# Recurrent attention with streamed weights: four stream buffers instead of six, thirteen streamed slices instead of fifteen, and three steps of the segment loop moved

## The chip, the cores and the metric

The kernel is written in Bass and Tile for Trainium2 and runs on one core. The metric is the device time of one execution in microseconds, as the median of three executions. The core has a tensor engine (PE, whose weight loads are listed apart as PEld), a vector engine (DVE), a scalar engine (ACT), GpSimd (POOL) and a sync engine (SP). SP computes nothing here: it issues the loads of the weights. ACT issues the other transfers of the loop that this document is about, between its own computations. Each engine works through its own instruction stream in order and waits on semaphores; a transfer is issued by an engine and then carried out by sixteen DMA engines.

## The reference, cut to what matters

```python
# part A: 64 segments of 32 tokens, with 8 memory rows handed from one to the next
for s in range(n_seg):                       # 2048 / 32 = 64
    h = concat([mem, x[:, 32*s:32*s+32]])    # 40 x 640
    q, k, v = h @ Wq, h @ Wk, h @ Wv         # each 640 -> 32 heads x 192
    p = softmax(mask(q @ k.T * 192**-0.5))
    o = (p @ v) @ Wo                         # 32 x 192 -> 640
    mem = o[:, :8]
    outs.append(o[:, 8:])
# part B: attention of 32 heads x 20 with a window of 8 keys, 2 apart
return g * a + (1 - g) * b                   # g = sigmoid(x . gate_w)
```

`outs` holds 40 - 8 = 32 rows a segment; the first eight rows of each segment's result are the memory of the next one. So the 64 segments form a chain: the first projection of a segment needs the last sums of the one before. The four matrices of part A (Wq, Wk, Wv and Wo, each 640 x 6144 in bf16) are needed in every segment.

## The kernel before

Three stages follow one another. **Part B** computes the windowed attention and leaves its result, already multiplied by 1 - g, in DRAM. **The prepass** (L409) computes the projections of the last eight tokens of each segment for all segments at once and leaves them in `zpk_dram`. **Part A** (L480) is the recurrence, one pass of `for s in range(nseg)` (L530) for each segment. After it `part_z` multiplies the rest of the rows by Wo.

**Weights.** Wq, Wk, Wv and Wo are cut into 80 slices of 128 x 1536 bf16, 384 KB each (`slice_keys`, L338). They don't all fit in the on-chip memory. `weights_setup` (L355) picks `N_STREAM` slices, spread evenly over an estimated time of use, that are loaded anew in every segment; the others stay resident, some loaded at the start (`wres_...`), `N_LATE` of them later (`wlate_...`). With `N_STREAM` = 15 the streamed ones are, in order of use, k(1,0), k(0,2), q(0,4), k(3,0), q(2,2), q(2,3), k(3,4), v(1,1), v(0,3), v(2,0), v(3,2), v(3,4), ob 2, ob 5 and ob 8; the numbers of q, k and v are a group of eight heads R and a chunk kc of the 640 inputs. `get_slice` (L404) loads a streamed slice through SP into one of `WBUFS` buffers (`wst`); SP issues these loads in order, and each waits until PE has done with the slice that had the buffer before. Streamed slices of Wo come from a rearranged copy in DRAM (`wscr`).

**Order.** In part A the order of PE, ACT and DVE is that of the program text (`manual_schedule`). One segment runs:

- `m_qk(0, ...)` and `m_qk(1, ...)`: q and k of head groups 0, 1 and 2, 3 with `m_dense` (L533), for each chunk kc four slices of four matmuls (a row of 32 PE columns each). Group pair 0 goes to the PSUM pairs `ps_d_5310` and `ps_d_5311`, pair 1 to `ps_d_5312` and `ps_d_5313`. After the last chunk ACT copies one pair out and DVE the other (L547).
- Between them stand parts of the previous segment. `sel_b` (L682, matmuls at L688, a copy at L692) sums chunks 2 to 4 of the next memory into `hT`, which the chunks kc = 2, 3, 4 of this segment read; chunks 0 and 1 were done by `sel("oa")` inside the previous segment. `tail` (L764, L768) forms the previous segment's output rows, `store` (L774) writes them out.
- `load_vz(s)` (L519): ACT issues the transfer of the prepass's V into `Vz`, columns 224 to 608 of the tile `ZQ`. The previous segment's `zst`, columns 32 to 416 of the same tile, is being written to `oz_dram` (L749), so this transfer has to wait for that one.
- `t_qk(0)` (L559): PE transposes q and k (L566), DVE copies Q^T (L569), ACT copies K^T (L570). Then the scores `s_a`, `s_b`, the exponentials (L602), and V with `m_v`.
- `pv_half(0)`, `pv_half(1)` (L629): attention times V, with copies by ACT and DVE at L652 and L657; `e_norm(1)` (L626, L627, on DVE) comes before `pv_half(1)`.
- `o_group(parts, i2)` (L669): the product with Wo, twelve groups of four rows of 128. Groups 0 to 5 do both column parts "oa" and "ob" (256 and 384 columns wide) at once, then 6 to 11 the part "oa", then 6 to 11 the part "ob". Groups 0 to 5 need only the first half of the heads; groups from 6 on need the copies at L652 that follow `pv_half(1)`. ACT copies the sums out at L746 ("oa") and L756 ("ob").

Of the kernel before, what the change touches and what calls it, by code (L numbers as in the profile page):

```python
# [11 lines left out]
F32 = mybir.dt.float32  # L12
I32 = mybir.dt.int32

N_STREAM = 15
N_LATE = 55
N_LATE2 = 11
WBUFS = 6

_DEV = {"mode": "full"}  # L20

# [2 lines left out]
QK = [[(m, R) for R in (2 * h, 2 * h + 1) for m in "qk"] for h in range(2)]  # L24
# [21 lines left out]
class _K:  # L46
# [308 lines left out]
    def weights_setup(self):  # L355
# [9 lines left out]
        self.stream_keys = set()  # L365
        for i in range(N_STREAM):
            left = [k for k in keys if k not in self.stream_keys]
            self.stream_keys.add(min(left, key=lambda k: abs(at[k] - (i + 0.5) * t / N_STREAM)))
        rest = [k for k in keys if k not in self.stream_keys]
# [10 lines left out]
        if so:  # L380
            scr = self.dram.tile([len(so), 128, 1536], BF, name="wscr")
            for i, k in enumerate(so):
                src, split = self.slice_info(k)
                nc.sync.dma_start(scr[i].rearrange("p (c f) -> p c f", c=split[0]), src)
                self.wscr[k] = scr[i]
        self.wstream = self.ctx.enter_context(tc.tile_pool(name="wstream", bufs=WBUFS))

# [92 lines left out]
    def part_a(self):  # L480
# [4 lines left out]
        with ctx:  # L485
# [20 lines left out]
            pairs = [psp.tile([128, 2, 512], F32, name=f"ps_d{b}") for b in range(4)]  # L506
# [11 lines left out]
            def load_vz(s):  # L518
                nc.scalar.dma_start(Vz, self.zpk_dram[s, :, 0:384])  # L519
# [10 lines left out]
            for s in range(nseg):  # L530
                pqs, sts, pSs = {}, {}, {}

                def m_dense(ks, kcs, dst):  # L533

                    for kc in kcs:
                        for x, k in enumerate(ks):
                            sl = self.get_slice((*k, kc))
                            for j in range(4):
                                mm = nc.tensor.matmul(dst[x // 2][32 * j:32 * j + 32, x % 2, 0:384], lhsT=hT[:, kc, :],  # L539
                                                      rhs=sl[:, 384 * j:384 * j + 384], start=(kc == 0),  # L540
                                                      stop=(kc == KC - 1), tile_position=(0, 32 * j),
                                                      skip_group_check=True)
                                if x:
                                    _LOADED.add(mm.ins.name)

                def copy_pair(cp, u, ps):
                    cp(KV[:, 384 * u:384 * u + 768].rearrange("p (a f) -> p a f", a=2), ps[:, :, 0:384])  # L547

                def m_qk(h, kcs):
                    dst = pairs[2 * h:2 * h + 2]  # L550
                    m_dense(QK[h], kcs, dst)
                    if kcs[-1] == KC - 1:
                        copy_pair(nc.scalar.copy, 0, dst[0])
                        copy_pair(nc.vector.tensor_copy, 2, dst[1])
# [4 lines left out]
                def t_qk(h):  # L559

                    pq, pk = (pairs[2 * h + m].bitcast(BF)[:, 0, 0:768].rearrange("p (r t f) -> p r t f", r=2, t=3)
                              for m in range(2))
                    for r in range(2):
                        for m, p in enumerate((pq, pk)):
                            for t in range(3):
                                nc.tensor.transpose(p[:, r, t, :], unit[2 * r + m][:, 128 * t:128 * t + 128],  # L566
                                                    self.ident[:])
                    blocks = lambda p: p.rearrange("p r t (j b i) -> p (r t j) b i", j=4, i=8)
                    nc.vector.tensor_copy(QTa[:, 2 - h:6 - h].rearrange("p b r c i -> p (r c) b i"), blocks(pq))  # L569
                    nc.scalar.copy(KV[:, 4 * 384:6 * 384].rearrange("p (c b i) -> p c b i", b=4, i=8), blocks(pk))  # L570
# [51 lines left out]
                def e_norm(h, rz):  # L622
                    E = Es[h]
                    EA = E[:, :, 0:80].rearrange("p a (r q) -> p a r q", q=40)
                    EB = E[:, :, 80:112].rearrange("p a (r q) -> p a r q", q=16)
                    nc.vector.tensor_tensor(out=EA, in0=EA, in1=rz, op=ALU.mult)  # L626
                    nc.vector.tensor_tensor(out=EB, in0=EB, in1=rz[:, :, :, 0:16], op=ALU.mult)  # L627
# [41 lines left out]
                def o_group(parts, i2):  # L669
                    for x, part in enumerate(parts):  # L670
                        n = 256 if part == "oa" else 384
                        for jj in range(4):
                            c = 4 * i2 + jj
                            R, j, t = c // 12, c // 3 % 4, c % 3
                            mm = nc.tensor.matmul(b_out[part][32 * jj:32 * jj + 32, 0:n],  # L675
                                                  lhsT=oTxs[2 * (R // 2) + j // 2][:, 6 * (j % 2) + 3 * (R % 2) + t, :],
                                                  rhs=o_weights(part, c), start=(c < 4), stop=(c >= 44),
                                                  tile_position=(0, 32 * jj), skip_group_check=True)
                            if x:
                                _LOADED.add(mm.ins.name)  # L680
# [12 lines left out]
                        "p (m i) -> p m i", i=8))  # L693

                m_qk(0, (0,))
                if sel_b is not None:
                    sel_b()
                if tail is not None:
                    tail()
                m_qk(0, (1, 2, 3))  # L700
                if store is not None:
                    store()
                    load_vz(s)
                m_qk(0, (4,))
                m_qk(1, (0, 1))
                t_qk(0)
                m_qk(1, (2, 3, 4))
                for chunks in (FULL, HALF):
                    s_a(0, chunks)
# [26 lines left out]
                nc.vector.tensor_copy(unit[2], pairs[3][:, 0, 0:384])  # L736
                nc.scalar.copy(unit[3], pairs[3][:, 1, 0:384])
                e_norm(1, rz)
                for i2 in range(4):
                    o_group(("oa", "ob"), i2)  # L740
                pv_half(1)
                for i2 in range(4, 6):
                    o_group(("oa", "ob"), i2)
                for i2 in range(6, 12):
                    o_group(("oa",), i2)
# [11 lines left out]
                if s + 1 < nseg:  # L757
                    def sel_b(hT_next=hT_next, sel=sel):
                        sel("ob", hT_next)

                def tail(s=s):
                    pa = pairs[2][:, 0, :]
                    for jj in range(4):
                        nc.tensor.matmul(pa[32 * jj:32 * jj + 32, 0:160], lhsT=self.sel_x[:],  # L764
                                         rhs=whi[:, 160 * jj:160 * jj + 160], start=True, stop=True,
                                         tile_position=(0, 32 * jj), skip_group_check=True)
                    g = self.gA[:, 16 * (s % 4) + s // 4:16 * (s % 4) + s // 4 + 1]
                    nc.vector.scalar_tensor_tensor(out=a4[:], in0=pa[:, 0:160], scalar=g, in1=a4[:], op0=ALU.mult,  # L768
                                                   op1=ALU.add)

                def store(s=s):
                    dst = self.out2d[32 * s:32 * s + 32, :].rearrange("t (j f) -> j t f", j=4)
                    if s + 1 < nseg:
                        nc.scalar.dma_start(dst, a4[:])  # L774
                    else:
                        for jj in range(4):
                            nc.scalar.dma_start(dst[jj, 0:24], a4[32 * jj:32 * jj + 24, :])
# [112 lines left out]
```

## Time and profile before

| | us |
|---|---|
| median of three executions | 1849.25 |
| lowest and highest | 1848.68 and 1857.12 |
| the profiled execution | 1856.27 |
| its span, first to last instruction | 1854.5 |
| part B | about 0 to 248 |
| prepass | about 248 to 435 |
| recurrence, 64 segments | about 435 to 1796 |
| `part_z` | about 1797 to 1854 |

A profile row names the engine, the line of the kernel and the operation, then the tile written and the tiles read (`ps_d_5311<-wst,hT` is a matmul of a streamed slice with the segment's input into a PSUM pair), the number of instructions and their time. What stands behind `<-` in square brackets or in the list of waits is what ended the idle time before. "issue" means that the engine waited for nothing that the profile shows. The streams named `q1`, `q10` and `q8` are the transfers that SP and ACT issue and the loading of program code.

### The profile page before, as it was taken

What the parts mean: (1) busy time and instruction counts of PE and PEld (TensorE: products, weight loads), DVE (VectorE), ACT (ScalarE), POOL (GpSimd) and SP (SyncE); (2) the same over time, 40 slices, a digit from 0 to 9 for tenths busy, and PEclk for the clock granted to TensorE, in tenths of its full rate; (3) what the DMA queues carried; (4) which work ended last, traced back from release to release, by engine and by line L of the source; (5) the groups of instructions that cost most, each with busy time, mean ns of one, the idle gap of its engine ahead of it and who ended that gap; (6) DMA issues with size and microseconds to landing.
All of it is one profiled execution on the core that took longest, in us unless ns stands there. A gap on an engine that the chain in (4) does not pass through costs nothing.

```text
span 1854.5 us, 79891 instructions
## 1 busy us (share of the span) xinstructions
PE 1642.1 (89%) x42080; PEld 751.1 (40%) x30176; DVE 781.2 (42%) x1663; ACT 766.7 (41%) x1417; POOL 41.0 (2%) x70
## 2 busy tenths in 40 slices
PE   3898898887998899998889989999888999899989
PEld 1455543332333334343333433333333333333348
DVE  2565578942333333333333443333433334333330
ACT  1675778942333333333333333333333333333340
POOL 3111000001000000000000000000000000000000
PEclk9999999998999999999999999999999999999989
DMA  9212179888999999999989998999998999899991
GB/s 279 34 44 48 33 189 284 160 169 266 312 301 303 301 312 330 313 317 307 303 301 312 319 315 293 301 311 315 312 308 284 321 311 319 296 309 313 312 298 29
DMA packets 340921, 486.15 MB, mean 262 GB/s; under 512 B 148964, under 2 KB 209892, under 8 KB 340580
## 3 DMA queue, kind: packets, MB, share of 16 engines
q1 hardware_dynamic: 198608, 419.28, 67.5%
q10 hardware_dynamic: 141972, 61.76, 14.2%
q8 instruction: 283, 4.64, 1.0%
q14 instruction: 58, 0.48, 0.1%
HBM read 446.61 MB, written 35.52 MB: 260 GB/s over the span
## 4 chain that ended last, share of the span: by engine, by line
PE 63%; DMA 15%; ACT 8%; DVE 6%; issue 6%; ACTq 2%; SPq 0%; POOL 0%; DVEq 0%
PE ps_d_5313 L539 11%; DMA oz_dram<-ZQ 10%; PE ps_d_5311 L539 9%; PE ps_d_5310 L675 6%; DVE ZS L94 5%; PE ps_d_5311 L675 5%; PE ps_d_5312 L539 5%; PE ps_bqk L240 2%; ACT bP L263 2%; PE ps_pre L441 2%; PE ps_d_5310 L539 2%; PE ps_d_5310 L566 2%; PE ps_d_5311 L821 2%; ACT KV L547 2%; PE ps_d_5312 L566 1%
## 5 line engine op out<-in xcount | busy, mean ns | idle before, releaser
L539 PEld LDWEIGHTS <-hT 128*32 128x32 bf16 x5120 | 137.6, 96 | 344.0 <-issue 246.1
L547 DVE CAST KV<-ps_d_5311 128x768 bf16<-128x768 f32 x128 | 122.6, 958 | 194.9 <-PE ps_d_5311 L539 194.9
L675 PEld LDWEIGHTS <-KV 128*32 128x32 bf16 x4608 | 131.7, 98 | 127.7 <-issue 65.4
L547 ACT CAST KV<-ps_d_5310 128x768 bf16<-128x768 f32 x64 | 51.1, 798 | 261.8 <-PE ps_d_5313 L539 58.0
L566 PEld LDWEIGHTS <-KV 128*128 128x128 bf16 x1536 | 87.2, 99 | 117.8 <-ACT KV L547 86.2
L92 ACT CAST ZS<-ps_pre 128x512 bf16<-128x512 f32 x48 | 123.9, 3048 | 11.9 <-DMA zpk_dram<-ZS 5.3
L94 DVE CAST ZS<-ps_pre 128x512 bf16<-128x512 f32 x48 | 123.4, 2944 | 10.5 <-DMA zpk_dram<-ZS 5.3
L539 PE MATMUL ps_d_5313<-wst,hT 128*32 128x384 bf16 x1280 | 110.9, 331 | 0.0
L547 DVE CAST KV<-ps_d_5313 128x768 bf16<-128x768 f32 x64 | 61.3, 958 | 105.0 <-PE ps_d_5313 L539 105.0
L641 PEld LDWEIGHTS <-KV 32*128 32x128 bf16 (+1 forms) x4096 | 49.2, 98 | 88.6 <-issue 31.8
L570 ACT COPY KV<-ps_d_5313 128x768 bf16<-128x768 bf16 x64 | 51.1, 799 | 74.9 <-PE ps_d_5313 L566 73.3
L652 DVE CAST KV<-ps_d_5313 128x384 bf16<-128x384 f32 x64 | 35.7, 558 | 107.3 <-PE ps_d_5313 L645 107.3
L570 ACT COPY KV<-ps_d_5311 128x768 bf16<-128x768 bf16 x64 | 51.1, 798 | 70.4 <-PE ps_d_5311 L566 70.4
L547 ACT CAST KV<-ps_d_5312 128x768 bf16<-128x768 f32 x64 | 51.1, 798 | 66.0 <-PE ps_d_5312 L539 64.7
L675 PE MATMUL ps_d_5311<-wst,KV 128*32 128x384 bf16 x768 | 75.9, 338 | 2.5 <-issue 2.4
L569 DVE COPY ZQ<-ps_d_5310 128x768 bf16<-128x768 bf16 x64 | 35.7, 558 | 91.8 <-PE ps_d_5310 L566 91.8
L539 PE MATMUL ps_d_5311<-wst,hT 128*32 128x384 bf16 x768 | 64.7, 327 | 9.7 <-DMA wst<-in_A_Wv_dram 9.7
L566 PE MATMUL ps_d_5310<-ident,KV 128*128 128x128 bf16 x384 | 43.7, 224 | 31.9 <-ACT KV L547 31.5
L652 ACT CAST KV<-ps_d_5310 128x384 bf16<-128x384 f32 x64 | 30.6, 479 | 99.3 <-PE ps_d_5312 L612 68.7
L652 ACT CAST KV<-ps_d_5312 128x384 bf16<-128x384 f32 x64 | 30.6, 478 | 90.3 <-PE ps_d_5313 L645 90.3
L652 DVE CAST KV<-ps_d_5311 128x384 bf16<-128x384 f32 x64 | 35.7, 558 | 75.8 <-PE ps_d_5312 L614 50.3
L263 ACT ACTIVATE bP<-ps_bS 128x968 bf16<-128x968 f32 (+1 forms) x80 | 64.7, 856 | 3.9 <-PE ps_bS L258 3.8
(689 smaller groups left out, 4351.7 us busy)
## 6 DMA issues: line engine op xcount, KB each, us to landing
wst<-in_A_Wv_dram SPq DMA_DIRECT2D x325, 384.0 KB
wst<-in_A_Wk_dram SPq DMA_DIRECT2D x260, 384.0 KB
wst<-in_A_Wq_dram SPq DMA_DIRECT2D x195, 384.0 KB
wst<-wscr SPq DMA_DIRECT2D x192, 384.0 KB
zpk_dram<-ZS ACTq DMA_DIRECT2D x8, 1536.0 KB
ZQ<-zpk_dram ACTq DMA_DIRECT2D x64, 192.0 KB
zpk_dram<-ZV ACTq DMA_DIRECT2D x32, 192.0 KB
ZQ<-zpk_dram ACTq DMA_DIRECT2D x64, 96.0 KB
```

The costliest lines, as they stand in the source:

```text
L92: nc.scalar.copy(out, in_)
L94: nc.vector.tensor_copy(out, in_)
L240: nc.tensor.matmul(ps[:, 0:nn], lhsT=wqk[n][:, kc, 4 * g:4 * g + 4, :].rearrange("p h d -> p (h d)"), rhs=xT[:, kc, o0:o0 + nn], start=(kc ...
L263: nc.scalar.activation(Pv, ps[0:nk, :, 0:nq * nu], ACT.Exp, scale=scale_b)
L441: nc.tensor.matmul(pss[g][:], lhsT=zT[:, kc, 128 * st:128 * st + 128], rhs=sls[kc][:, 512 * g:512 * g + 512], start=(kc == 0), stop=(kc == ...
L539: mm = nc.tensor.matmul(dst[x // 2][32 * j:32 * j + 32, x % 2, 0:384], lhsT=hT[:, kc, :], rhs=sl[:, 384 * j:384 * j + 384], start=(kc == 0 ...
L547: cp(KV[:, 384 * u:384 * u + 768].rearrange("p (a f) -> p a f", a=2), ps[:, :, 0:384])
L566: nc.tensor.transpose(p[:, r, t, :], unit[2 * r + m][:, 128 * t:128 * t + 128], self.ident[:])
L570: nc.scalar.copy(KV[:, 4 * 384:6 * 384].rearrange("p (c b i) -> p c b i", b=4, i=8), blocks(pk))
L641: nc.tensor.matmul(out[:, r, t, :], lhsT=V[2 * h + r][ks, f0:f1], rhs=E[ks, par, 40 * r:40 * r + 40], start=(r == 0 and t == 0), stop=Fals ...
L652: cp(oTxs[2 * h + jp].rearrange("p (j c) q -> p j c q", j=2), src[:, :, :, 8:40])
L675: mm = nc.tensor.matmul(b_out[part][32 * jj:32 * jj + 32, 0:n], lhsT=oTxs[2 * (R // 2) + j // 2][:, 6 * (j % 2) + 3 * (R % 2) + t, :], rhs ...
```

## The change

The number of streamed slices goes from 15 to 13 and the number of stream buffers from six to four: two buffers' memory holds two more resident slices. Because the choice is spread anew, other slices are streamed: k(1,0), k(1,2), k(1,4), k(3,1), q(3,2), q(3,4), v(1,1), v(1,3), v(3,0), v(2,3), oa 1, oa 3 and ob 8. Twelve slices instead of ten are loaded at the start, ahead of the first four (instead of six) streamed ones.

Within a segment three things move. The chunk kc = 1 of q and k of the first pair is split: its slices for `ps_d_5310` now stand ahead of `sel_b` and `tail`, those for `ps_d_5311` behind. `load_vz(s)` moves from behind `store` to behind `t_qk(0)`, and so on ACT's stream behind the copy of K^T. The fourth `o_group` moves from ahead of `pv_half(1)` to behind it.

```diff
-N_STREAM = 15
+N_STREAM = 13
-WBUFS = 6
+WBUFS = 4
...
                 m_qk(0, (0,))
+                m_dense(QK[0][0:2], (1,), pairs[0:1])
                 if sel_b is not None:
                     sel_b()
                 if tail is not None:
                     tail()
-                m_qk(0, (1, 2, 3))
+                m_dense(QK[0][2:4], (1,), pairs[1:2])
+                m_qk(0, (2, 3))
                 if store is not None:
                     store()
-                    load_vz(s)
                 m_qk(0, (4,))
                 m_qk(1, (0, 1))
                 t_qk(0)
+                if s > 0:
+                    load_vz(s)
                 m_qk(1, (2, 3, 4))
...
-                for i2 in range(4):
+                for i2 in range(3):
                     o_group(("oa", "ob"), i2)
                 pv_half(1)
-                for i2 in range(4, 6):
+                for i2 in range(3, 6):
                     o_group(("oa", "ob"), i2)
```

## The prediction

> **What bounds the kernel now.** I read the page first, then the instructions of one line, the busy time by stretches, the chain that ended last within the recurrence, the waits of PE, and the timeline of a few segments.
>
> ```profile
> PE 1642.1 (89%) x42080; PEld 751.1 (40%) x30176; DVE 781.2 (42%) x1663; ACT 766.7 (41%) x1417; POOL 41.0 (2%) x70
> ```
> ```profile
> q8 instruction: 283, 4.64, 1.0%
> ```
> ```profile
> L746 ACT CAST ZQ<-ps_d_5310 x64: 372/372/373, 468.7 to 1793.2; 128x256 bf16<-128x256 f32 x64
> ```
> ```profile
> 1040.00:1240.00 200.00, 181.54 (x5534) 76.69 (x3775) 76.59 (x202) 72.24 (x164) 0.00 (x0) 0.98 0.92 307
> ```
> ```profile
> 1797.00:1855.00 58.00, 53.51 (x1533) 49.06 (x1525) 6.38 (x12) 8.19 (x6) 0.00 (x0) 0.97 0.20 59
> ```
>
> L746 runs once a segment, so a segment takes (1793.2 - 468.7) / 63 = 21.0 us, and 64 of them are nearly three quarters of the span. In a stretch of 200 us there (columns: PE, PEld, DVE, ACT, POOL, granted clock, DMA share, GB/s) PE is busy for 181.5 and the next engine for 76.6: the recurrence is bound by PE and by what stops PE. The DMA engines are busy for 0.92 of the time; in `part_z` for 0.20.
>
> The chain that ended last, between 460 and 1790 us, and PE's waits in the same window:
>
> ```profile
> by line: PE ps_d_5313 L539 15.2%; DMA oz_dram<-ZQ 13.8%; PE ps_d_5311 L539 12.3%; PE ps_d_5310 L675 8.2%; PE ps_d_5311 L675 6.9%; issue 6.5%; PE ps_d_5312 L539 6.4%; PE ps_d_5310 L539 2.7%; PE ps_d_5310 L566 2.3%; ACT KV L547 2.2%; PE ps_d_
> ```
> ```profile
> PE ps_d_5310 L566 <- ACT KV L547: 26.9, 33, 2.5
> ```
> ```profile
> PE ps_d_5311 L539 <- DMA wst<-in_A_Wv_dram: 2.5, 2, 1.9
> ```
>
> Two things stop PE. The first has a name: `t_qk(0)` waits for ACT's copy of q and k, 26.9 us in 33 segments. The second is "issue", 6.5% of 1330 us = 86 us. For the streamed weights PE waits 2.5 us in all, so the loads as such bound nothing.
>
> What "issue" is can be counted. The page gives 283 code packets of 4.64 MB, 16.4 KB each; PE has 42080 + 30176 = 72256 instructions, 255 for each packet. Three idle times in a row, and the stretches between their ends:
>
> ```profile
> 1073.62 0.39 PE L675 MATMUL ps_d_5310<-wlate_oa_4126,KV 128*32 128x256 bf16 x5 [1.63 <-issue]
> ...
> 1095.48 0.34 PE L675 MATMUL ps_d_5311<-wlate_ob_5252,KV 128*32 128x384 bf16 x3 [1.14 <-issue]
> ...
> 1113.54 0.40 PE L675 MATMUL ps_d_5311<-wlate_ob_5244,KV 128*32 128x384 bf16 x2 [2.23 <-issue]
> ```
> ```profile
> 1073.60:1095.47 21.87, 19.65 (x604) 8.43 (x418) 7.94 (x21) 7.87 (x18) 0.00 (x0) 1.00 0.90 302
> 1095.47:1113.53 18.06, 15.76 (x465) 6.15 (x301) 7.22 (x19) 6.51 (x14) 0.00 (x0) 1.00 0.96 316
> ```
>
> PE runs 604 + 418 = 1022 instructions between the first two and 465 + 301 = 766 between the next, and with the semaphore instructions that are not counted that is 4 and 3 times 256. So PE stands still because the next 256 instructions have not arrived, and it does so where they are shortest. [...]
>
> **The change part by part.** The sum is made against the profiled execution, 1856.27 us (span 1854.5), which lies 7.0 above the median of 1849.25.
>
> *V's load behind the K^T copies.* The mechanism in one early segment, from the chain, and the ACT rows of a later one:
>
> ```profile
> 469.11 4.76 DMA oz_dram<-ZQ
> 473.94 0.33 ACTq L519
> 474.32 0.81 ACT KV L547
> 475.17 0.34 PE ps_d_5310 L566 x3
> ```
> ```profile
> 1074.95 1.24 ACTq L749 DMA_DIRECT2D oz_dram<-ZQ  x1
> ```
> ```profile
> 1082.11 0.80 ACT L570 COPY KV<-ps_d_5311 128x768 bf16<-128x768 bf16 x1 [1.59 <-PE ps_d_5311 L566]
> 1083.91 0.80 ACT L547 CAST KV<-ps_d_5312 128x768 bf16<-128x768 f32 x1 [1.00 <-PE ps_d_5312 L539]
> ```
> ```profile
> 1580.19 6.82 DMA oz_dram<-ZQ
> ```
>
> ACT stands at the trigger of L519 until the store of `oz_dram` has landed, the copy L547 is queued behind it, and the transposes wait for the copy. After the change the trigger stands behind L570, whose end (1082.91) is 6.7 us after the store's trigger ended (1076.19). The longest landing in the chain is 6.82 (with the trigger's own time in it), the one above 4.76, so the trigger finds the store done. What is then queued behind it, the next L547, starts 1.00 us after L570 ends, and the trigger takes 0.33. V's prepass rows are first read in `pv_half(0)`, several us later. I take the whole 26.9: **-27**, bounds -27 and 0.
>
> *Thirteen slices, fewer bytes.* Within 460 to 1790 us:
>
> ```profile
> q1 hardware_dynamic: 139556, 375.14, 83.2%
> ```
>
> q1 is the stream. Two slices in fifteen less take 83.2 x 2/15 = 11 points off a share of 0.92, leaving 0.81, or 0.83 on a shorter segment. No load waits are there to be saved (2.5 us); what can be saved is the code's wait in the queue. At a share of 0.20 `part_z` executes 1533 + 1525 instructions without an idle time worth naming (53.5 of 58 us busy), at 0.92 there are 86 us. On a straight line between these two, 0.09 less share is worth 86 x 0.09 / 0.72 = 11 us. If what counts is the idle share of the DMA engines, it doubles from 0.08 to 0.17 and the wait halves, 43 us. Both are estimates; I take the middle, **-27**. The ends are -86 (all gone) and +5: the segment has four weight loads more (below) and comes round faster, so that as much code is due in less time.
>
> [...]
>
> *Four buffers.* A load may start when the slice four places back has been used. The shortest such stretch in the new order is k(1,2) to q(3,4), in this segment from 1078.70, when PE leaves k(1,2), to 1083.81, the start of the pair that holds q(3,4):
>
> ```profile
> 1078.37 0.33 PE ps_d_5311 L539 x8
> ...
> 1083.81 0.33 PE ps_d_5313 L539 x8
> ```
> ```profile
> 1389.15 3.17 DMA wst<-in_A_Wq_dram
> ```
> ```profile
> 1776.50 6.83 DMA wst<-in_A_Wv_dram
> ```
>
> That is about 5 us. Of the loads that the chain names as long pieces in this window, one took 3.17 us and one, beside the four loads of `oz` ahead of `part_z`, 6.83. So there is some 1.8 us left, and I cost it at **0**. If the cover goes, the wait is whatever a load takes beyond 5 us, at most 6.83 - 5.1 = 1.7 us a segment.
>
> *Next-memory sums later.* The rows around `sel_b`:
>
> ```profile
> 1077.09 0.22 PE L688 MATMUL ps_d_5313<-sel_m,ZQ 128*32 128x8 bf16 x12
> ...
> 1077.56 0.33 PE L539 MATMUL ps_d_5311<-wres_q_1_72,hT 128*32 128x384 bf16 x4
> ...
> 1077.72 0.10 PEld L539 LDWEIGHTS <-hT 128*32 128x32 bf16 x4 [0.46 <-DVE hT L692]
> ```
>
> From the start of `sel_b` to the weight load that needs its result 1077.72 - 1077.09 = 0.63 us pass, through DVE's copy L692. PE fills them now with `sel_b`, `tail` and the four slices of chunk 1, the third of which starts at 1077.56. After the change only two slices are left behind `sel_b`, and PE is done with them 1077.56 - 1077.09 = 0.47 after its start. The two slices that go ahead fill nothing: all of chunk 0, which waits for ACT's L756, still stands in front. So PE loses 0.16 us in 63 segments: **+10**, bounds 0 and +16 (0.26 each, if the load's 0.10 is not covered). Splitting chunk 1 loads `hT` once more, four weight loads of 0.10 beside matmuls: 0.
>
> *Fourth group behind `pv_half(1)`.*
>
> ```profile
> 1070.15 0.33 PE L675 MATMUL ps_d_5311<-wlate_ob_5248,KV 128*32 128x384 bf16 x4
> 1070.41 0.19 PE L641 MATMUL ps_d_5312<-ZQ,KV 32*128 32x40 bf16 x2
> ...
> 1071.37 0.34 PE L675 MATMUL ps_d_5311<-wst,KV 128*32 128x384 bf16 x4
> 1071.71 0.28 PE L675 MATMUL ps_d_5310<-wlate_oa_4126,KV 128*32 128x256 bf16 x1
> ```
> ```profile
> 1070.10 0.21 DVE L627 TENSOR_TENSOR ZQ<-ZQ,ps_d_5312 128x64 bf16<-128x64 bf16 x1
> ```
>
> Groups come every 0.27 us. The fourth ends as L627 does, at 1070.31, so ahead of `pv_half(1)` it fills a wait; moved, it leaves 0.27 empty there and fills the 0.18 ahead of group 6 (1071.71, against 1071.53 where matmuls 0.16 apart would go on). That loses 0.09 in 64 segments, 6 us; where PE comes late from a code stall it wins up to 0.18. I take **+3**, bounds -12 and +6.
>
> Start, prepass and `part_z` hold the same sixteen early loads (ten and six, now twelve and four), two streamed loads fewer, and otherwise the same work: 0, give or take 4.
>
> Sum: -27 - 27 + 10 + 3 = -41. 1856.3 - 41 = 1815, and less the 7.0 that the profiled execution lies above the median: **1808 us**.
>
> **The rivals.** [...]
>
> *Code stalls mostly go*: if they need a full queue, 70 of the 86 us vanish, -27 - 70 + 13 = -84, 1765 us.
>
> *Four buffers are too few* (slower): at q(3,4) a load that takes more than 5 us stops PE. The other terms are worth 41 / 64 = 0.64 us a segment, so it decides from 5.7 us on; at the longest row's 6.83 it costs 1.7 x 64 = 109, and 1849 - 41 + 109 = 1917. A load of 6 us, half way, would cost 58 and give 1866. Against it: 2.5 us of waits today and a row of 3.17; for it: the share is still above 0.8, and the code, the store and V's load, which now falls into this stretch, share the engines.
>
> **How the numbers follow.** Chances: forecast 0.47, code waits as before 0.25, code stalls mostly gone 0.16, too few buffers 0.12. The range takes in the first two with their bounds and the upper half of the third: 1770 to 1842. Within 0.5% is 1840 to 1858.5, about what a measurement of this kernel can tell from no change. Of the second case 0.07 lies there, of the fourth 0.04. So faster 0.81, same 0.11, slower 0.08.
>
> **What would show it.** PE's wait at L566 for ACT's L547 should fall to a few us; L519 should follow L570 with no idle time; "issue" in the chain should fall from 6.5% to about 4.5%; the DMA share in the recurrence to about 0.83; a PE gap of 0.16 us for DVE's L692 should appear at the third chunk. PE waits for `wst` of more than 10 us, or an "issue" share that has not moved, would make the prediction wrong.

## The result and the profile after

| | before | after |
|---|---|---|
| median, us | 1850.56 (4 runs) | 1782.29 (4 runs) |
| lowest and highest, us | 1848.68 and 1857.12 | 1779.47 and 1786.32 |
| ratio, 95% interval | | 0.9627, 0.9593 to 0.966 |
| profiled execution and its span, us | 1856.27, 1854.5 | 1779.78, 1778.0 |

The change is worth 68 us in the medians, where 41 were forecast. In the profiled executions the spans differ by 76.5 us, since the one before lies 5.7 us above its median and the one after 2.5 below. The page's head after the change, and the instructions of ACT's copy of the "oa" sums, which runs once a segment (L749 now, L746 before):

```profile
span 1778.0 us, 79937 instructions
...
PE 1619.1 (91%) x42065; PEld 756.6 (43%) x30432; DVE 780.6 (44%) x1663; ACT 767.8 (43%) x1417; POOL 41.1 (2%) x70
```
```profile
L749 ACT CAST ZQ<-ps_d_5310 x64: 372/373/374, 465.0 to 1715.0; 128x256 bf16<-128x256 f32 x64
```

From the first segment's copy to the last one's it takes 1715.0 - 465.0 = 1250.0 us, against 1324.5 before: 74.5 of the 76.5 us come from the recurrence, 1.18 us a segment. Start and end give the other 2.

The waits of PE between 480 and 1650 us, a window that leaves out the first and the last segments (engine, tile and line, what it waited for: us in total, times, longest). Before, the two longest:

```profile
PE ps_d_5310 L566 <- ACT KV L547: 23.6, 29, 2.5
PE ps_d_5310 L675 <- issue: 18.0, 14, 2.5
```

After:

```profile
PE ps_d_5311 L539 <- ACT ZQ L759: 12.0, 29, 0.9
PE ps_d_5310 L675 <- issue: 8.6, 15, 1.1
PE ps_d_5312 L641 <- DVE ZQ L627: 8.5, 51, 0.2
PE ps_d_5313 L539 <- DMA wst<-in_A_Wq_dram: 3.5, 10, 0.9
```

The wait for L547 is gone from the list. All rows with "issue" add up to 66.9 us before and 24.2 us after, the longest single one 2.5 before and 1.1 after. Waits for `wst` are new in this window, 6.8 us. Outside it they are 3.5 us in the last segments (2.5 before) and one of 12.3 us in the first segment, where one of 7.2 stood before. The wait of `pv_half(1)` for DVE's L627 is new too.

Busy time, clock and DMA in the same stretch of 1000 us (columns as in the prediction), before and then after:

```profile
600.00:1600.00 1000.00, 909.64 (x27632) 383.36 (x18764) 380.39 (x1003) 358.14 (x812) 0.00 (x0) 0.99 0.93 309
```
```profile
600.00:1600.00 1000.00, 951.34 (x29286) 409.50 (x20066) 400.31 (x1057) 378.35 (x856) 0.00 (x0) 1.00 0.90 288
```

The reader is to see three things. PE does 6% more matmuls in the same time. The granted clock goes from 0.99 to 1.00. And the DMA share falls only from 0.93 to 0.90, while the bytes fall by 7%.

For a closer look I split each segment at PE's first instruction of a phase, from the records of the trace, and took the mean over 63 segments. In us:

| stretch of a segment | before | after | V's load alone (e1) | streams alone (e2) | no stream at all (e7) |
|---|---|---|---|---|---|
| ACT's copy of "ob" to `t_qk(0)` | 5.49 | 5.20 | 5.06 | 5.50 | 5.09 |
| `t_qk(0)` to `pv_half(0)` | 7.89 | 8.03 | 7.90 | 7.97 | 7.77 |
| `pv_half(0)` to the copy of "ob" | 7.68 | 6.64 | 8.00 | 6.64 | 6.23 |
| sum, parts rounded | 21.06 | 19.87 | 20.96 | 20.12 | 19.10 |

Nearly nine tenths of the gain (1.04 of 1.19) lie in the row from `pv_half(0)` to the copy of "ob", the stretch with the most instructions per us, which neither the move of V's load nor that of the sums touches. The move of the fourth group lies in it, but the streams alone (e2) bring the same 6.64 without it.

### The profile page after: what moved, and what is told of

It reads as the page before. It is cut to its first block, busy times and chain, and to the rows that moved or that the text cites. A ratio compares the mean times of both kernels' runs of the same rounds, so it can differ in the third digit from the quotient of the medians.

```text
span 1778.0 us, 79937 instructions
## 1 busy us (share of the span) xinstructions
PE 1619.1 (91%) x42065; PEld 756.6 (43%) x30432; DVE 780.6 (44%) x1663; ACT 767.8 (43%) x1417; POOL 41.1 (2%) x70
## 4 chain that ended last, share of the span: by engine, by line
PE 66%; DMA 12%; DVE 8%; ACT 6%; issue 5%; ACTq 2%; SPq 0%; POOL 0%; DVEq 0%
PE ps_d_5313 L539 12%; PE ps_d_5311 L539 11%; DVE ZS L94 5%; PE ps_d_5312 L539 5%; PE ps_d_5310 L675 4%; PE ps_d_5311 L675 4%; PE ps_d_5310 L539 4%; DMA wst<-in_A_Wq_dram 4%; PE ps_bqk L240 2%; ACT bP L263 2%; PE ps_pre L441 2%; DMA wst<-in_A_Wk_dram 2%; PE ps_d_5311 L824 2%; DMA wst<-in_A_Wv_dram 2%; PE ps_d_5312 L566 1%
## 5 line engine op out<-in xcount | busy, mean ns | idle before, releaser
L539 PEld LDWEIGHTS <-hT 128*32 128x32 bf16 x5376 | 142.4, 95 | 373.8 <-issue 282.3
L547 DVE CAST KV<-ps_d_5311 128x768 bf16<-128x768 f32 x128 | 122.6, 958 | 174.1 <-PE ps_d_5311 L539 174.0
L675 PEld LDWEIGHTS <-KV 128*32 128x32 bf16 x4608 | 128.0, 95 | 85.4 <-issue 39.8
L547 ACT CAST KV<-ps_d_5310 128x768 bf16<-128x768 f32 x64 | 51.1, 799 | 205.3 <-PE ps_d_5310 L539 198.0
L539 PE MATMUL ps_d_5313<-wst,hT 128*32 128x384 bf16 x1280 | 108.6, 328 | 19.7 <-DMA wst<-in_A_Wq_dram 17.6
L566 PEld LDWEIGHTS <-KV 128*128 128x128 bf16 x1536 | 86.7, 98 | 89.0 <-ACT KV L547 52.3
L547 DVE CAST KV<-ps_d_5313 128x768 bf16<-128x768 f32 x64 | 61.3, 957 | 124.2 <-PE ps_d_5313 L539 124.2
L539 PE MATMUL ps_d_5311<-wst,hT 128*32 128x384 bf16 x1280 | 107.7, 326 | 3.9 <-DMA wst<-in_A_Wv_dram 2.4
L641 PEld LDWEIGHTS <-KV 32*128 32x128 bf16 (+1 forms) x4096 | 53.1, 97 | 80.7 <-DVE ZQ L607 29.8
L547 ACT CAST KV<-ps_d_5312 128x768 bf16<-128x768 f32 x64 | 51.2, 799 | 67.7 <-PE ps_d_5312 L539 67.7
L675 PE MATMUL ps_d_5310<-wst,KV 128*32 128x256 bf16 x768 | 72.4, 272 | 4.4 <-issue 4.4
L585 PEld LDWEIGHTS <-KV 128*32 128x32 bf16 (+1 forms) x4096 | 45.9, 92 | 67.7 <-issue 50.1
L652 ACT CAST KV<-ps_d_5310 128x384 bf16<-128x384 f32 x64 | 30.7, 479 | 84.4 <-PE ps_d_5312 L612 73.9
L692 DVE CAST hT<-ps_d_5313 128x24 bf16<-128x24 f32 x63 | 11.5, 183 | 114.5 <-PE ps_d_5312 L767 112.1
```

The lines of the kernel that those rows point to most:

```text
L585: nc.tensor.matmul(pSs[h][32 * j:32 * j + 32, par, 40 * r:40 * r + 40], lhsT=KT[R][k0:k1, c, :], rhs=q_blocks(R)[k0:k1, :, c, :], start=(r ...
L641: nc.tensor.matmul(out[:, r, t, :], lhsT=V[2 * h + r][ks, f0:f1], rhs=E[ks, par, 40 * r:40 * r + 40], start=(r == 0 and t == 0), stop=Fals ...
L652: cp(oTxs[2 * h + jp].rearrange("p (j c) q -> p j c q", j=2), src[:, :, :, 8:40])
```

## The experiments

The theory (A) after the result: V's load held up ACT and through it PE; the traffic of the stream held up PE's code; fewer bytes in a shorter queue let the code arrive earlier; the moves of the sums and of the fourth group are worth little. Its rivals are that the pause at the transposes only moves, that the code waits as long whatever is queued, and that the reordering is the gain.

### One part at a time: e1 to e4

e1 is the kernel before with V's load moved, e2 the kernel before with the new numbers of slices and buffers. e3 is the changed kernel with the sums put back, e4 the changed kernel with the fourth group put back.

```diff
 e1 (to the kernel before)
                     store()
-                    load_vz(s)
...
                 t_qk(0)
+                if s > 0:
+                    load_vz(s)
 e2 (to the kernel before)
-N_STREAM = 15
+N_STREAM = 13
-WBUFS = 6
+WBUFS = 4
 e3 (to the changed kernel)
-                m_dense(QK[0][0:2], (1,), pairs[0:1])
...
-                m_dense(QK[0][2:4], (1,), pairs[1:2])
-                m_qk(0, (2, 3))
+                m_qk(0, (1, 2, 3))
 e4 (to the changed kernel)
-                for i2 in range(3):
+                for i2 in range(4):
...
-                for i2 in range(3, 6):
+                for i2 in range(4, 6):
```

> The kernel before with one edit: V's load is triggered behind the K^T copy. Theory A (V's load held ACT, ACT held the transposes): PE's idle time at L566 for ACT's L547 goes from 26.9 us to under 3, the time falls by about 25 us (ratio near 0.986), the code stalls stay near 86 us of issue in the chain. Rival B (the pause only moves, because code and weights that arrived in it are then late): L566's wait goes and issue or waits for wst grow by as much, ratio within 0.995 to 1.0.

> The kernel before with only the thirteen streamed slices in four buffers. Theory A (less queued traffic lets code arrive earlier): PE's stalls at 256-instruction boundaries fall by about half, from some 75 us of plain idle time to some 40, the half-clock windows of 3.4 us in the recurrence go from nine to two or fewer, and the time falls by 40 to 55 us (ratio 0.970 to 0.978). Rival B (code waits its turn whatever is queued, and the gain of the whole change came from the reordering): ratio 0.99 or above, issue in the chain as before.

> The changed kernel with the next-memory sums put back ahead of chunk 1. Theory A (two slices behind them are too few to cover DVE's copy into hT): the stretch from ACT's copy of the ob sums to the first transposes gets shorter by 0.10 us a segment, 6 us in all, so 1776 us against the change's 1782 (ratio to before 0.959). Rival B (the move pays, since it gives ACT and DVE more time): the time rises by 5 us or more, ratio above 0.966.

> The changed kernel with the fourth group of the product with Wo put back ahead of pv_half(1). Theory A (clean segments lose 0.09 us by the move, segments with a late PE win up to 0.18): within 6 us of 1782, either way (ratio 0.960 to 0.966). Rival B (the move pays whenever PE waits for ACT's copies, in every segment): the time rises by 0.18 x 64 = 12 us, ratio 0.969.

| | median, us | ratio to before, 95% interval |
|---|---|---|
| e1, V's load alone | 1845.52 | 0.9957, 0.9924 to 0.9991 |
| e2, streams alone | 1793.09 | 0.9682, 0.9648 to 0.9716 |
| e3, the change without the sums' move | 1778.24 | 0.9594, 0.9558 to 0.9631 |
| e4, the change without the group's move | 1786.62 | 0.9643, 0.9601 to 0.9685 |

**e1** goes to rival B nearly whole. PE's waits in e1 between 480 and 1650 us (this profile lists the PSUM pairs under one name):

```profile
PE ps_d L675 <- issue: 30.7, 24, 2.4
PE ps_d L641 <- issue: 25.6, 26, 1.7
PE ps_d L645 <- issue: 19.4, 14, 2.5
```

The wait at L566 for L547 is gone, as expected. But "issue" adds up to 84.2 us against 66.9, and in the table above the last stretch grows from 7.68 to 8.00 us while the first shrinks from 5.49 to 5.06. Of 0.43 us a segment that the transposes gain, 0.32 come back where the code is late. This trace is of the slowest of the twelve executions (1854.93 us, the median is 1845.52), so the median one may give back less. The time falls by some 8 us (0.43% of 1852, interval 2 to 14), not by 25.

**e2** goes to theory A. The three longest waits of PE:

```profile
PE ps_d L566 <- ACT KV L547: 22.1, 35, 1.1
PE ps_d L675 <- issue: 15.7, 23, 1.5
PE ps_d L539 <- ACT ZQ L756: 10.8, 21, 0.8
```

The wait for L547 is as long as before, "issue" is down to 28.5 us. None of the nine stretches at half clock that the trace of before has (below) is left. The streams alone bring 59 of the 68 us, and were even a little underrated in the expectation (40 to 55).

**e3**: the stretch from the copy of "ob" to the transposes is 5.12 us against 5.20 with the sums moved, so the move costs 0.08 x 63 = 5 us in its place; the medians differ by 4 us, which the intervals don't separate. e3 is also e2 with V's load and the fourth group moved: 1778.24 against 1793.09, 15 us, and the intervals of the two don't meet. So with less traffic these two moves bring some 15 us, where V's load alone brought 8 in e1, and still not the 24 us that L566's 22.1 us of waiting in e2 come to over 64 segments. In the changed kernel the wait for the sums is plain. Before, the row in question started 0.16 us after its neighbour:

```profile
1077.72 0.33 PE L539 MATMUL ps_d_5311<-wlate_k_1_4060,hT 128*32 128x384 bf16 x4
1077.88 0.33 PE L539 MATMUL ps_d_5310<-wres_q_2_74,hT 128*32 128x384 bf16 x4
```

After:

```profile
1058.90 0.22 PE L688 MATMUL ps_d_5313<-sel_m,ZQ 128*32 128x8 bf16 x12
1058.98 0.23 PE L767 MATMUL ps_d_5312<-ZQ,sel_x 128*32 128x160 bf16 x4
1059.05 0.33 PE L539 MATMUL ps_d_5311<-wres_q_1_72,hT 128*32 128x384 bf16 x4
1059.21 0.33 PE L539 MATMUL ps_d_5311<-wlate_k_1_4062,hT 128*32 128x384 bf16 x4
1059.45 0.35 PE L539 MATMUL ps_d_5310<-wres_q_2_74,hT 128*32 128x384 bf16 x4
```

Slices follow at 0.16; the one at 1059.45 comes 0.24 after its neighbour, 0.08 late.

**e4**: within the 6 us of theory A, and its interval overlaps that of the change. In e4 the wait for L627 is gone (8.5 us in the changed kernel), but "issue" is 31.1 us against 24.2. In a quick segment (the fifth percentile of 64) the first group is 3.50 us ahead of the copy of "oa" after the change and 3.48 in e4, so what the moved group leaves empty ahead of `pv_half(1)` it fills again behind it, but for 0.02 us. Whether the move helps or harms the time stays open; it is small.

### Bytes, buffers and code: e5, e6, e7 and e10

e5 has fifteen streamed slices in four buffers, e10 fourteen in five (`N_STREAM` and `WBUFS` alone, in the changed kernel). e6 leaves out the loading of six of the thirteen streamed slices of the recurrence, e7 of all of them: a resident slice stands in their place, so PE runs the same instructions on other weights and the products are not the reference's.

```diff
 e6; in e7 the condition is True
+        if getattr(self, "in_loop", False):
+            self.skip_n = getattr(self, "skip_n", -1) + 1
+            if self.skip_n % 2 == 1:
+                sub = {"q": ("q", 0, 0), "k": ("k", 0, 0), "v": ("v", 0, 0), "oa": ("oa", 0), "ob": ("ob", 0)}[key[0]]
+                return self.res_tiles[sub]
         return self.load_slice(self.wstream, key, "wst", "wst")
```

> The changed kernel with fifteen streamed slices again, but in four buffers: the bytes of before, the queue depth of after. Theory A (the bytes load the DMA engines, and code waits in proportion): stalls of code grow towards those of before, issue over 60 us, and PE begins to wait for wst; 1830 us or more (ratio 0.985 to 1.0). Rival B (what counts is how many loads may queue, four buffers against six): issue stays near the change's 25 us of plain idle time, ratio below 0.972.

> The changed kernel with six of the thirteen streamed slices of the recurrence left out (a resident slice is used in their place, so these products are not the reference's). Theory A: with the stream's bytes nearly halved, the stalls at 256-instruction boundaries fall from some 49 us (start to start, in the records) to under 15, and the time to about 1740. [...]

> The changed kernel with all thirteen streamed slices of the recurrence left out (resident slices in their place, so these products are not the reference's). Both theories: almost no code stalls are left, issue under 5 us, about 1725 us; this is what the stream costs in all. If issue stays above 20 us, code does not wait for the stream at all, and both are wrong.

> The changed kernel with fourteen streamed slices in five buffers, half way back. Theory A (code stalls follow the traffic): the waits for wst in the recurrence vanish but for the one at the start, issue in PE's waits lies between the change's 25 us and 91 us, some half-clock windows return; about 1800 to 1815 us (ratio 0.972 to 0.980). Rival B (it was the buffers' tightness or the reordering, not the traffic): ratio below 0.965.

DMA share and rate between 600 and 1600 us, PE's waits between 480 and 1650 us (sums of the rows), in us:

| | slices, buffers | DMA share, GB/s | "issue" | waits for `wst` | median | ratio, 95% interval |
|---|---|---|---|---|---|---|
| e1 | 15, 6 | 0.93, 312 | 84.2 | 0 | 1845.52 | 0.9957, 0.9924 to 0.9991 |
| before | 15, 6 | 0.93, 309 | 66.9 | 0 | 1850.56 | |
| e10 | 14, 5 | 0.91, 301 | 50.9 | 0.4 | 1808.03 | 0.9786, 0.9739 to 0.9832 |
| e5 | 15, 4 | 0.91, 299 | 29.0 | 67.0 | 1896.18 | 1.0262, 1.021 to 1.0313 |
| after | 13, 4 | 0.90, 288 | 24.2 | 6.8 | 1782.29 | 0.9627, 0.9593 to 0.966 |
| e6 | 7, 4 | 0.62, 173 | 7.8 | 0 | 1738.69 | 0.9401, 0.934 to 0.9462 |
| e7 | 0, 4 | 0.12, 31 | 0 | 0 | 1719.71 | 0.9299, 0.9239 to 0.9359 |

The waits that remain in e7 are all of them:

```profile
PE ps_d L546 <- ACT ZQ L766: 18.3, 23, 1.2
PE ps_d L648 <- DVE ZQ L634: 9.7, 60, 0.2
```

(L546 and L648 are the lines called L539 and L641 elsewhere, seven further down.) With the stream gone, PE executes the same code, and no "issue" is left in 1170 us. So the stalls are code that waits for the stream, as theory A has it for e6 and e7. That it is code is also counted for all of them now: the 68 idle times with "issue" before end at the places 193 to 195 modulo 256 in PE's instructions, semaphore instructions included, and the 50 after at the places 178 to 180. From a DMA share of 0.93 before to 0.90 after, these idle times fell from 66.9 to 24.2 us, so the code did not wait as long as before.

In the records of the code packets the same is seen from the other side. The time from PE's crossing of one 256-instruction boundary to the start of the next code packet has a median of 1.95 us before, 1.79 after, 1.16 in e6 and 0.58 in e7. Where PE stalled it was 2.54 us before and 1.98 after, and PE went on 2.39 us after the packet's start in both (all medians). In e7, where nothing stalls, PE runs 66.5 instructions a us from `pv_half(0)` to the copy of "ob", so 256 of them last 3.85 us. A packet that starts after 2.54 us is then 2.54 + 2.39 - 3.85 = 1.1 us too late, one after 1.98 only 0.5. That fits the idle times: 68 of 0.98 us in the mean before, 50 of 0.48 after. Here 0.56 us less delay goes with a mean stall half as long, because the code arrives just about when it is needed.

e5 answers to neither expectation in full. It is slower than before, as A had it and further, but its "issue" is low, as B had it. PE's longest waits in e5:

```profile
PE ps_d L539 <- DMA wst<-in_A_Wv_dram: 35.3, 44, 1.9
PE ps_d L539 <- DMA wst<-in_A_Wq_dram: 17.8, 34, 1.3
PE ps_d L539 <- DMA wst<-in_A_Wk_dram: 11.3, 19, 2.0
```

With fifteen slices in four buffers the weights are late instead of the code. So the smaller queue alone is no gain: it pays only together with the two slices less. Because PE stands waiting for weights in e5, its low "issue" can't say whether the queue's depth by itself lets code through. e10 came out as theory A had it, 1808 us between before and after. e10 against after points to the depth (0.91 and 0.90 of DMA share, but 50.9 and 24.2 us of "issue", with five and four buffers), yet both number and depth change between them. The code packets speak for the other side. Nine tenths of them start within 3.05 us of the crossing before, 2.99 in e5 and 3.06 in e10, but 2.63 after and 2.55 in e2. By this fifteen slices make the code as late in four buffers as in six, which would make it the bytes and not the depth. But with 2.76 us e9, the run with the fewest slices of these, doesn't follow the bytes, and where PE waits for weights (70.9 us in e9) its crossings may fall at other times. So the question is left open.

### Trying for more: e8, e9 and e11

PE's longest wait after the change is for ACT's copy of the "ob" sums (L759, 12.0 us of plain idle time). e8 puts two chunks of the first PSUM pair in front of it, which don't need that copy, and leaves four slices behind the sums. e9 adds the next step in buffers, twelve slices in three. e11 keeps thirteen in four and picks other slices.

```diff
 e8 (to the changed kernel)
-                m_qk(0, (0,))
-                m_dense(QK[0][0:2], (1,), pairs[0:1])
+                m_dense(QK[0][0:2], (0, 1), pairs[0:1])
...
-                m_dense(QK[0][2:4], (1,), pairs[1:2])
+                m_dense(QK[0][2:4], (0, 1), pairs[1:2])
 e9 (to e8)
-N_STREAM = 13
+N_STREAM = 12
-WBUFS = 4
+WBUFS = 3
 e11 (to e8): k(0,1), k(1,2), k(1,4), k(3,1), k(3,2), k(3,4), v(1,1), v(0,4), v(3,0), v(2,3), ob 2, oa 3, ob 8
```

> The changed kernel with chunks 0 and 1 of q(0), k(0), q(1)... of the first pair split once: both chunks of the first PSUM pair ahead of the next-memory sums, both of the second behind. Theory A (PE waits for ACT's copy of the ob sums with too little work in front of it, and then for DVE's copy into hT): 0.3 us of the first wait and 0.1 to 0.2 of the second go, 0.5 x 63 = 31 us at most, some of it given back to code stalls; 1752 to 1765 us (ratio 0.946 to 0.953). Rival B (all is given back, as with V's load alone): ratio above 0.959.

> The kernel of the run e8 (chunks 0 and 1 split once around the sums) with twelve streamed slices in three buffers: the next step along the same trade of buffers for residents. Theory A (with four buffers the loads already land only 1.6 us ahead of their use, against 3.1 us that a load takes): three buffers leave about 4.5 us for a load at the mean and less at the tight places, PE waits for wst by 1 us or more a segment, and what code stalls give back does not pay for it; 1790 us or more (ratio above 0.967). Rival B (less traffic also shortens the loads, so that three buffers do): ratio below 0.955.

> The kernel of e8 (both chunks of a PSUM pair together around the sums) with the same number of streamed slices and buffers, but the thirteen chosen by the times of use measured in e8, so that the shortest stretch for a load grows from 4.9 to 5.3 us. Theory A (what e8 saved at the sums came back as waits for the stream at the tight places): the waits for q(3,2) and q(3,4) go, some 0.2 us a segment of the 0.29 that e8 gave back, 1764 to 1770 us (ratio 0.952 to 0.957). Rival B (the stream as a whole is at its limit, wherever its slices lie): the waits move to other slices and the ratio stays at 0.959 or above.

| | median, us | ratio to before, 95% interval |
|---|---|---|
| e8 | 1777.38 | 0.9612, 0.9574 to 0.9651 |
| e9 | 1833.71 | 0.9911, 0.988 to 0.9942 |
| e11 | 1776.65 | 0.9601, 0.9557 to 0.9644 |

e8 was a miss: in its place it gains (from the copy of "ob" to the transposes 4.95 us against 5.20 in the mean, 4.69 against 5.09 in the tenth percentile), but its time can't be told from that of the change. Its waits between 480 and 1650 us show where the rest went:

```profile
PE ps_d L675 <- issue: 11.9, 16, 1.3
PE ps_d L641 <- DVE ZQ L627: 8.5, 51, 0.2
PE ps_d L539 <- DMA wst<-in_A_Wq_dram: 7.7, 18, 1.5
...
PE ps_d L688 <- ACT ZQ L758: 3.7, 10, 0.5
```

The dense slices no longer wait for ACT's copy (L758 here), but the sums behind them do, 3.7 us instead of 12.0; waits for the stream come to 11.1 us against 6.8, "issue" to 29.5 against 24.2. So all of the 12.0 comes back, as rival B had it. e11 moves the waits for the stream from Wq to Wk, and the time stays, as rival B had it (its lines L673 and L537 are L675 and L539 elsewhere):

```profile
PE ps_d L673 <- issue: 9.6, 17, 1.0
PE ps_d L537 <- DMA wst<-in_A_Wk_dram: 8.8, 20, 1.1
```

e9 shows the other end of the trade, as theory A expected. PE waits for weights in nearly every segment:

```profile
PE ps_d L539 <- DMA wst<-in_A_Wk_dram: 37.5, 58, 1.8
PE ps_d L539 <- DMA wst<-in_A_Wv_dram: 21.6, 41, 1.7
```

Of the four pairs 15 and 6 (e1 and before, both in the old order), 14 and 5 (e10), 13 and 4, 12 and 3 (e9, in the order of e8, which by itself costs nothing), the change's is the best measured. No run that loads all its weights beats the changed kernel by more than the intervals allow; e3, e8 and e11 lie 4 to 6 us below it.

## Why the prediction came out as it did

The direction and the two causes were right, and 1782 lies in the range; two terms of the sum were not, and their errors partly cancel. 1782 is nearer to the 1765 of the rival that the code stalls mostly go than to the forecast's 1808. Step by step:

- *V's load behind the K^T copies*, -27. The mechanism is as described. The ACT rows after the change have the trigger right behind the copy, with nothing waited for:

```profile
1063.70 0.80 ACT L570 COPY KV<-ps_d_5311 128x768 bf16<-128x768 bf16 x1 [1.60 <-PE ps_d_5311 L566]
1063.76 0.33 ACTq L519 DMA_DIRECT2D ZQ<-zpk_dram  x1
1065.50 0.80 ACT L547 CAST KV<-ps_d_5312 128x768 bf16<-128x768 f32 x1 [1.00 <-PE ps_d_5312 L539]
```

  In its place it is worth the forecast 27 us. But the terms were added as if they were independent, and this one isn't: under the old traffic it brings 8 us (e1), and with the new streams some 15 together with the fourth group (e3 against e2). What e1 gains at the transposes stands again in "issue"; that the quicker segment calls for its code sooner is the likely reason, which no run shows by itself. The case "code waits as before", with 0.25 of the chances and its part of the range, rested on a wait that less traffic does not shorten. That was an assumption of mine, which no run shows: "issue" fell from 66.9 to 24.2 us. It also counted V's load in full, 27 less 13 for the two other moves, which makes 1835 us; e1 shows that this was too hopeful.
- *Thirteen slices, fewer bytes*, -27: the step that was mis-sized. Plain "issue" fell from 66.9 to 24.2 us in the window, or, for 64 segments of 21.06 and 19.87 us, from 77 to 26: -51. The DMA share that I had reckoned with, 0.83, did not come; it is 0.90, and by the straight line I drew 0.03 of share would be worth 4 us. The stalls hang on something finer than the share: half a microsecond in the start of the code packets where PE stalls, 2.54 us after the crossing before and 1.98 after.
- *What had no term*: nine of the long pauses went with a lower clock too. In this window before the change the clock record has nine stretches of 3.4 us at half speed, and none after; at half of 3.4 us each that is up to 15 us. Eight of them come with an idle time with "issue" of 1.5 to 2.4 us, one with the wait of 2.5 us for L547; two start 0.6 and 0.2 us before that idle time ends, seven 0.1 to 1.2 us after. PE's busy time for a segment fell from 19.16 to 18.90 us (its share between 600 and 1600 us, times 21.06 and 19.87), 16 us in 64, which agrees. One of the nine in the trace of before, right behind the stall of 2.23 us at 1113.54:

```profile
1113.60:1117.00 3.40, 3.40 (x90) 1.60 (x72) 0.66 (x2) 0.62 (x2) 0.00 (x0) 0.51 0.43 125
```

  PE is busy for all of the 3.40 us, at a clock of 0.51. This side of a pause does not show in a list of waits.
- *Four buffers*, 0: nearly right. The waits for `wst` came to 6.8 us in the window, 10.3 from 460 us to the end of the recurrence, and one of 12.3 us in the first segment, where a wait of 7.2 us had stood before. The forecast had named more than 10 us as a sign that it is wrong. That sign was just reached, and did not mean what it was set for: these waits cost some 8 us more than before and did not decide. e5 and e9 show how close this is to the edge: one step on, or two slices more, and it is the bound. The rival was priced rightly in kind, and did not decide.
- *Next-memory sums later*, +10: right in sign in the traces, 0.08 to 0.10 a segment instead of 0.16, so 5 to 6 us (e3); the times don't separate it from zero.
- *Fourth group*, +3: can't be told from zero: e4 and the change differ by 0.0016 in the ratio, and each ratio is known to some 0.004. In quick segments it costs 0.02 us each, 1 us in all.

Together, in the spans: -27 - 51 - 15 + 7 + 6 + 1 = -79, against the 76.5 by which they fell. That is an account of idle and slow time in two traces, not of causes: what the moves saved came back in part as "issue", and by the runs with parts alone the streams bring 59 of the 68 us. The forecast's list of what would show it holds for L566, for L519 and for the gap behind L692; "issue" is 5.0% of the chain between 400 and 1720 us, near the 4.5% named, though PE's own waits for it fell by much more; and the DMA share did not fall to 0.83.

## What to carry to other kernels

Where an engine stands idle for "issue", count its instructions between the ends of these idle times. Here all 68 ended at three neighbouring places modulo 256, it was code that was late, and less traffic helped: 66.9 us of these waits with fifteen streamed slices in six buffers, 24.2 with thirteen in four, none with no stream. A wait removed elsewhere was then worth less than its length, 8 us here instead of 27 and some 15 once the traffic had been cut: don't add the two terms as if they were independent. And buffers against resident data was here a trade with a best point between two walls, late code on one side (fourteen in five, 50.9 us of "issue" and 1808.03 us) and late data on the other (twelve in three, 70.9 us of waits for `wst` and 1833.71 us): measure a step to either side.

## What the runs showed of the hardware that was not expected

- The DMA share did not follow the bytes. With 8% fewer bytes on the stream (281.08 MB in 1000 us before, 258.37 after) its share fell only from 83.0% to 79.3%: the mean packet of that queue took 134 ns (79.3% of 16 x 1000 us over 94598 packets) against 129 (83.0% over 102921).
- Pauses of PE of 1.5 to 2.5 us went with 3.4 us at half clock in nine cases of the recurrence before the change, in the window from 480 to 1650 us, but thirteen other pauses of 1.4 to 2.5 us did not.
